# Copies of V on GpSimd in place of SyncE transfers, and two tiles each of q/k and of exponentials turned by transfer

## The chip, the cores and the metric

One core of one Trainium2 chip. The kernel is one program on that core; its engines are TensorE (PE, with its weight loads shown as PEld), VectorE (DVE), ScalarE (ACT), GpSimd (POOL) and SyncE (SP), and 16 DMA engines move data for them. The metric is the device time of one launch in microseconds, lower is better: the median of the runs of one kernel.

## The reference

Attention with a few global rows beside a sliding window, followed by a two-layer network with a hard-swish-like activation. There are 8 batches, 8 heads, 512 local and 32 global positions, heads of 64 numbers. In float32:

```python
k_all = np.concatenate([k_g, k_l], axis=2)
v_all = np.concatenate([v_g, v_l], axis=2)
out_g = np.matmul(sm(scale * np.matmul(q_g, k_all.transpose(0, 1, 3, 2))), v_all)
s_ll = np.where(np.abs(pos[:, None] - pos[None, :]) <= 32, scale * q_l @ k_l^T, -1e9)
s_l = np.concatenate([scale * q_l @ k_g^T, s_ll], axis=-1)
out_l = np.matmul(sm(s_l), v_all)
x = concatenate([out_g, out_l], axis=2)   # to rows of (batch, position), 512 wide: 4352 x 512
h = x @ w_in                               # 512 -> 2048
out = (h * np.clip(h + 3.0, 0.0, 6.0) / 6.0) @ w_out   # 2048 -> 512
```

Here `sm` is a softmax over the last axis. A local position sees the 32 global keys and the local keys at most 32 positions away, so a run of 32 queries needs 32 + 96 = 128 keys.

## The kernel before

**Tiling.** A batch's 512 local positions are four tiles (j = 0 to 3) of 128. A tile's 128 queries are four runs (u = 0 to 3) of 32. For each run the 128 keys are the 32 global ones and a strip of 96 local ones that starts 32 positions before the run. All work on TensorE is in fp16 with fp32 sums.

**Loads.** GpSimd issues the loads, since they convert fp32 to fp16 on the way: q and k of a tile into `nat` (`load_qk`, line 425; 8 buffers), V of a batch into `ve` (`load_v`, line 477; two buffers, one for even and one for odd batches), the global rows into `natg`, and the two weight matrices `win` and `wout` in four pieces each (lines 560 to 566). All go through line 411. At most eight transfers of one queue are under way; the next issue waits for the one eight places before.

**Turning q and k.** `turn_qk` (line 578) makes the transposed form `qk`. For the batches before `TURN_QK` = 4 this is eight TensorE transposes (line 592) and a copy out of PSUM by ScalarE or VectorE (lines 296 and 298); from batch 4 on it is one transposing transfer issued by SyncE (line 582).

**Strips of V.** The second matmul of attention needs, for each run u of each tile, a weight tile whose 128 partitions hold the 32 global rows of V and the 96 local ones of that run. It lies in `st` (two buffers). `strips_moved` (line 526) fills it for a whole batch by seven SyncE transfers from `ve` (line 536): one spread of the 32 global rows to all 16 slots (4 runs x 4 tiles), then for each u the 96 rows, in one or two pieces as they cross a tile's border. With 32 global rows in front, u = 0 moves rows 0 to 95 to partitions 32 to 127; u = 1 moves rows 32 to 127 to partitions 32 to 127, the same ones; u = 2 and u = 3 come in two pieces each. Batch 0 is filled otherwise (`strips_kept` and the two-tile form) and the change doesn't touch it.

**A local step** (`local_step`, line 635): scores of one tile for all heads into PSUM `s` (lines 662 and 669), a masked minimum and bias by VectorE (line 681), exponentials with their sums by ScalarE (line 692), a reciprocal and a scaling into `pn` by VectorE (lines 702 and 706), then the transposition of `pn` into `et`: for the batches before `TURN_E` = 5 eight TensorE transposes (line 713) and one copy out of PSUM, from batch 5 on one SyncE transposing transfer (line 724). Then the matmul with the strips (line 743) into PSUM `a`, copied to `xt`. `global_steps` (line 772) does the 32 global queries of a batch; its last matmuls (line 848) read `ve` directly.

**The network.** `first` (line 863) multiplies by w_in (line 870), applies relu and scale on ScalarE (line 877) and a minimum and product on VectorE (line 881). `second` (line 887) multiplies 16 pieces by w_out into one PSUM bank of 512 columns (line 892), one copy to `ot` (3 buffers), one store. `moe_local` does one batch, `moe_global` all global rows at the end.

**The order.** The operations are not written in the order they run. Each is handed to a planner (`Plan.add`) with an engine, or two to choose from, a duration, what it depends on, a key (its due place) and the buffers it takes. `Plan.lay` walks through time by these durations and a model of the transfers, and gives each engine its list; `fill` adds idle matmuls to the first microseconds. So a changed duration or engine of one operation can move others, on every engine, and choose ScalarE or VectorE anew for each copy out of PSUM. On the chip each engine runs its list in order and waits on semaphores.

Of the kernel before, what the change touches and what calls it, by code (L numbers as in the profile page):

```python
# [79 lines left out]
class Plan:  # L80
# [128 lines left out]
def kernel(  # L209
# [12 lines left out]
    nc = tc.nc  # L222
# [303 lines left out]
    def strips_moved(b, js, key):  # L526
        r = b % 2
        n = len(js)
        j0, j1 = js[0], js[-1] + 1
        v4 = st[r].rearrange("p (u j) c -> p u j c", u=NU)  # L530
        before = [av_last[b - 2, j] for j in range(NJ)] if b >= 2 else []
        o = []

        def move(dst, src, packets, ns, deps):
            def emit(op):
                nc.sync.dma_start(out=dst, in_=src)
            o.append(add("SP", 600, emit, deps + before, key=key + 0.001 * len(o), dma=(packets, ns)))
# [12 lines left out]
        for c in range(NU):  # L550
            lo = c * UQ
            a = min(P - lo, KL)
            deps = [x for j in range(j0, j1) for x in vload[b, j]]
            move(v4[G:G + a, c, j0:j1, :], ve[b % VE][lo:lo + a, j0:j1, :], a * each, ns, deps)
            if a < KL:
                deps = [x for j in range(j0 + 1, j1 + 1) for x in vload[b, j]]
                move(v4[G + a:P, c, j0:j1, :], ve[b % VE][0:KL - a, j0 + 1:j1 + 1, :], (KL - a) * each, ns, deps)
        return o
# [14 lines left out]
            return []  # L573
        return [S_op[b - 2, jj] for jj in range(max(j - 1, 0), min(j + 1, NJ - 1) + 1)] + gS_op[b - 2]

    TURN_M, TURN_QK, TURN_E, TURN_G, TURN = 1, 4, 5, 5, (64, 190.0, True)

    def turn_qk(b, j, ld, key, which=(0, 1)):
        r = b % 2
        if b >= TURN_QK:  # L580
            def move(op):
                nc.sync.dma_start_transpose(out=qk[r][:, :, :, UQ + j * P:UQ + (j + 1) * P].rearrange(
                    "d i p s -> d (i p) s"), in_=nat[ld[0].slot].rearrange("s i c -> s (i c)"))
            return add("SP", 1250, move, [*ld, prep["clear"], *old_qk(b, j)], key=key, rel=ld[:1], dma=TURN)
        w0, n = which[0], len(which)

        def pe(op):
            ps = psM[op.slot].bitcast(FP16) if b < TURN_M else psT[op.slot]
            for i in which:
                for p in range(NP):  # L590
                    c0 = ((i - w0) * NP + p) * P
                    nc.tensor.matmul(out=ps[:, c0:c0 + P], lhsT=nat[ld[0].slot][:, i, p * P:(p + 1) * P],
                                     rhs=ident, is_transpose=True)
# [41 lines left out]
    def local_step(b, j, key):  # L635
# [75 lines left out]
        def tr(op):  # L711
            for h in range(H):
                nc.tensor.matmul(out=psT[op.slot][:, h * P:(h + 1) * P], lhsT=pn[pn_op.slot][:, h, :],  # L713
                                 rhs=ident, is_transpose=True)
        if b < TURN_E:
            t = add("PE", 450, tr, scs, key=key - 0.2, acq="T", rel=[pn_op])
            et_op = add("DVE", 0, lambda op: None, [t], key=key - 0.3, acq="et")

            def ev(op):
                copy(op, et[et_op.slot].rearrange("k h q -> k (h q)"), psT[t.slot])  # L720
            e_ = add(BOTH, (900, 600), ev, [et_op], key=key - 2, rel=[t])
        else:
            def move(op):
                nc.sync.dma_start_transpose(out=et[op.slot], in_=pn[pn_op.slot].rearrange("q h k -> q (h k)"))
            e_ = et_op = add("SP", 1250, move, scs, key=key - 2, acq="et", rel=[pn_op], dma=TURN)
# [158 lines left out]
                                           op0=ALU.min, op1=ALU.mult)  # L884
        return add("DVE", 600, st_, [a], key=key - 1, rel=[f, to])

    def second(t0, gdone, set_, dests, keys):
        f = None
        for q in range(4):
            def pe(op, q=q):  # L890
                for c in range(q * 4, q * 4 + 4):
                    nc.tensor.matmul(out=psM[(f or op).slot], lhsT=gs[set_.slot][:, c, t0:t0 + P],  # L892
                                     rhs=w_out_t[:, c, :], start=(c == 0), stop=(c == NDFF - 1))
            deps = gdone[q * 4:q * 4 + 4] + [wo[q * 4]]
            if q == 0:
                f = s = add("PE", 865, pe, deps, key=keys[q], acq="M")
            else:
                s = add("PE", 865, pe, deps + [s], key=keys[q], rel=[set_] if q == 3 else [])
        oo = add("DVE", 0, lambda op: None, [s], key=keys[3] - 1, acq="ot")

        def ev(op):
            copy(op, ot[oo.slot], psM[f.slot])
        c = add(BOTH, (480, 605), ev, [oo], key=keys[3] - 1, rel=[f])

        for n, (dst, lo, hi) in enumerate(dests):
            def sto(op, dst=dst, lo=lo, hi=hi):
                nc.sync.dma_start(out=dst, in_=ot[oo.slot][lo:hi, :])
            add("SP", 600, sto, [c], key=keys[3] + 0.001 * n, rel=[oo], dma=(hi - lo, STORE))

    def moe_local(b, at, span):  # L910
        set_ = add("ACT", 0, lambda op: None, xdone[b, 0], key=at - 1, acq="gs")
# [4 lines left out]
        def key():  # L916
            left[0] += 1
            return at + span * left[0] / 32
# [5 lines left out]
                done[part][c:c + k] = [o] * k  # L924
        for j in range(NJ):
            row = b * S + G + j * P
            second(j * P, done[j // per], set_, [(out[row:row + P, :], 0, P)], [key() for _ in range(4)])

    def moe_global(at, span):
        deps = [xgd[b] for b in range(B)]  # L930
# [122 lines left out]
```

## Time and profile before

| | us |
|---|---|
| median of 3 runs (lowest, highest) | 332.98 (332.3, 334.16) |
| the profiled execution | 335.23 |
| its span from first to last instruction | 333.5 |
| TensorE busy | 317.4 |
| VectorE busy | 265.2 |
| ScalarE busy | 253.9 |
| GpSimd busy | 106.1 |

The page counts an engine as busy from an instruction's start to its end; matmuls overlap, so the mean duration of one (379 ns for 512 columns) is longer than its share of the time (four take 0.86 us in the chain of waits). GpSimd's busy time is nearly all issuing of loads: 40 of V's local rows at 822 ns, 30 each of q and k at 899 and 914 ns. SyncE's issues aren't counted as busy. Transfers of the GpSimd queue carry 17.05 MB and take 71.9% of the 16 DMA engines' span, those of the SyncE queue 34.55 MB and 48.0%; together over 100%, since a packet's time includes waiting for packets of the other queue. The strips are 7 transfers of 512 KB, 14 of 384 KB, 14 of 256 KB and 14 of 128 KB for the batches 1 to 7, landing some 8 us after their issue. The granted TensorE clock is 0.999.

### The profile page before, as it was taken

To read this page: it belongs to the slowest core of one execution; us is meant where nothing else is said; L and a number is where in the kernel's file an instruction comes from. 1 tells how busy PE (TensorE), PEld (TensorE's weight loads), DVE (VectorE), ACT (ScalarE), POOL (GpSimd) and SP (SyncE) were. 2 spreads that over 40 slices of the span, in tenths; PEclk is the share of its full clock that TensorE was granted. 3 is DMA by queue.
4 is the path that set the end of the run, shared out by engine and by line. 5 is a ranking of instruction groups with operands and counts; after the bars stand their busy time and mean duration, and the time that the engine had idled before them with its cause. 6 is when DMAs were issued, how large, how long until landed. Compare 5 with 4: busy or idle time off the path is not lost.

```text
span 333.5 us, 10205 instructions
## 1 busy us (share of the span) xinstructions
PE 317.4 (95%) x3808; PEld 183.0 (55%) x3808; DVE 265.2 (80%) x997; ACT 253.9 (76%) x850; POOL 106.1 (32%) x139
## 2 busy tenths in 40 slices
PE   8989969799699999999999999999999999999995
PEld 6778855365356554555555555454455544546642
DVE  4899799789988799898998799689988896375400
ACT  4889798679789589977995689699988994474402
POOL 8724943198166733830760050005000000000000
PEclk9999999999999999999999999999999999999999
DMA  9999999999999999999999999999984215300022
GB/s 150 193 245 168 131 177 254 168 190 194 206 152 188 231 155 156 191 225 231 162 173 218 224 160 209 196 198 175 194 145 120 63 35 112 88 0 2 31 64 95
DMA packets 158594, 52.25 MB, mean 157 GB/s; under 512 B 142928, under 2 KB 151120, under 8 KB 158544
## 3 DMA queue, kind: packets, MB, share of 16 engines
q0 software_dynamic: 106560, 17.05, 71.9%
q1 hardware_dynamic: 51984, 34.55, 48.0%
q8 instruction: 30, 0.49, 0.6%
q14 instruction: 20, 0.16, 0.2%
HBM read 35.26 MB, written 8.91 MB: 132 GB/s over the span
## 4 chain that ended last, share of the span: by engine, by line
PE 60%; DMA 19%; POOL 7%; ACT 6%; DVE 5%; issue 2%; SPq 0%; ACTq 0%
PE m L892 28%; PE m L870 23%; DMA wout<-in_moe_w_out_dram 7%; DMA win<-in_moe_w_in_dram 5%; DMA nat<-in_k_l_dram 4%; POOL nat L411 3%; PE a L743 3%; POOL ve L411 3%; ACT sm L692 2%; DMA nat<-in_q_l_dram 2%; DVE gs L881 2%; PE s L669 2%; ACT t L877 1%; PE t L713 1%; PE s L662 1%
## 5 line engine op out<-in xcount | busy, mean ns | idle before, releaser
L892 PE MATMUL m<-wout,gs 128*128 128x512 f16 x544 | 129.6, 379 | 1.3 <-DMA wout<-in_moe_w_out_dram 1.3
L870 PE MATMUL m<-xt,win 128*128 128x512 f16 (+1 forms) x576 | 122.0, 355 | 1.7 <-DVE gs L881 1.0
L692 ACT ACTIVATE sm<-sm,stat 128x128 f32<-128x128 f32 x256 | 100.6, 397 | 11.4 <-DVE stat L681 10.8
L881 DVE SCALAR_TENSOR_TENSOR gs<-t,m 128x512 f16<-128x512 f32 x136 | 91.7, 683 | 19.6 <-ACT t L877 18.3
L877 ACT ACTIVATE t<-m 128x512 f32<-128x512 f32 x136 | 80.4, 597 | 22.1 <-PE m L870 21.3
L870 PEld LDWEIGHTS <-win 128*128 128x128 f16 x640 | 59.3, 98 | 52.2 <-issue 3.3
L892 PEld LDWEIGHTS <-gs 128*128 128x128 f16 x544 | 49.6, 98 | 52.7 <-issue 2.8
L681 DVE CUSTOM_DVE_ANT_0 sm<-s,mask 128x128 f32<-128x128 f32 x256 | 61.8, 283 | 2.5 <-PE s L669 1.1
L692 ACT ACTIVATION_READ_ACCUMULATOR sm<-sm,stat 128x1 f32 x256 | 49.6, 194 | 0.0
L706 DVE TENSOR_TENSOR pn<-sm,stat 128x512 f16<-128x512 f32 x64 | 44.0, 688 | 0.6
L411 POOL DMA_DIRECT2D ve<-in_v_l_dram x40 | 32.2, 822 | 15.0 <-PE m L870 4.3
L296 ACT CAST xt<-a 64x256 f16<-64x256 f32 (+1 forms) x83 | 31.0, 374 | 7.3 <-PE a L743 6.3
L411 POOL DMA_DIRECT2D nat<-in_q_l_dram x30 | 27.0, 899 | 23.1 <-DMA qk<-nat 10.2
L411 POOL DMA_DIRECT2D nat<-in_k_l_dram x30 | 27.4, 914 | 15.7 <-DMA nat<-in_k_l_dram 6.5
L743 PEld LDWEIGHTS <-st 128*128 128x128 f16 x448 | 19.7, 98 | 10.6 <-DVE et L298 0.3
L296 ACT COPY ot<-m 128x512 f32<-128x512 f32 x23 | 13.5, 588 | 13.8 <-PE m L892 10.5
L743 PE MATMUL a<-et,st 128*128 128x64 f16 x448 | 22.1, 193 | 0.2 <-ACT xt L296 0.2
L411 POOL DMA_DIRECT2D ve<-in_v_g_dram x8 | 4.8, 597 | 54.3 <-PE a L848 53.6
L681 DVE DVE_READ_ACCUMULATOR2_ANT stat<- 128x1 f32 x256 | 21.1, 83 | 0.0
L298 DVE CAST xt<-a 64x256 f16<-64x256 f32 (+1 forms) x33 | 14.1, 428 | 4.3 <-PE a L743 4.0
L702 DVE RECIPROCAL stat<-stat 128x4 f32<-128x4 f32 x64 | 11.1, 173 | 5.8 <-ACT sm L692 5.2
L807 ACT ACTIVATE sg<-a,stat 128x32 f32<-128x32 f32 x16 | 4.6, 287 | 14.3 <-DVE stat L798 14.3
(88 smaller groups left out, 279.6 us busy)
## 6 DMA issues: line engine op xcount, KB each, us to landing
out_dram<-ot SPq DMA_DIRECT2D x32, 256.0 KB, 3.7
st<-ve SPq DMA_DIRECT2D x14, 384.0 KB, 7.9
nat<-in_k_l_dram POOLq DMA_DIRECT2D x30, 128.0 KB, 8.1
nat<-in_q_l_dram POOLq DMA_DIRECT2D x30, 128.0 KB, 9.5
st<-ve SPq DMA_DIRECT2D x7, 512.0 KB, 7.7
st<-ve SPq DMA_DIRECT2D x14, 256.0 KB, 8.0
ve<-in_v_l_dram POOLq DMA_DIRECT2D x24, 128.0 KB, 6.0
st<-ve SPq DMA_DIRECT2D x18, 128.0 KB, 8.0
```

Of the source, the lines that this page charges most:

```text
L296: nc.scalar.copy(out=out, in_=in_)
L298: nc.vector.tensor_copy(out=out, in_=in_)
L411: nc.gpsimd.dma_start(out=dst(op), in_=src)
L681: nc.vector.tensor_tensor_reduce(out=sm[sm_op.slot][:, h, :], in0=psS[s.slot][:, e, p * P:(p + 1) * P], in1=m, scale=-scale, scalar=3.0e38 ...
L692: nc.scalar.activation(out=sm[sm_op.slot][:, h, :], in_=sm[sm_op.slot][:, h, :], func=EXP, scale=-1.0, bias=stat[stat_op.slot][:, 0, h:h + 1],
L702: nc.vector.reciprocal(out=stat[stat_op.slot][:, 2, h0:h1], in_=stat[stat_op.slot][:, 1, h0:h1])
L706: (nc.gpsimd if op.eng == "POOL" else nc.vector).tensor_tensor(out=pn[pn_op.slot][:, h0:h1, :], in0=sm[sm_op.slot][:, h0:h1, :], in1=stat[ ...
L743: nc.tensor.matmul(out=psA[a][:, c0:c0 + 64], lhsT=st[r][:, u * NJ + j, p * P:(p + 1) * P], rhs=et[et_op.slot][:, 2 * p:2 * p + 2, u * UQ: ...
L870: nc.tensor.matmul(out=psM[op.slot][:, i * n:(i + 1) * n], lhsT=w_in_t[:, m, (c + i) * P:(c + i + 1) * P], rhs=x()[:, m, t0:t0 + n], start ...
L877: nc.scalar.activation(out=t1[to.slot], in_=psM[f.slot], func=RELU, bias=0.5, scale=1.0 / 6.0)
L881: nc.vector.scalar_tensor_tensor(out=gs[set_.slot][:, c:c + k, t0:t0 + n], in0=t1[to.slot].rearrange("f (k t) -> f k t", k=k), scalar=1.0, ...
L892: nc.tensor.matmul(out=psM[(f or op).slot], lhsT=gs[set_.slot][:, c, t0:t0 + P], rhs=w_out_t[:, c, :], start=(c == 0), stop=(c == NDFF - 1))
```

## The change

- In `strips_moved`, for a whole batch (batches 1 to 7), the spread of the global rows is no transfer any more but eight GpSimd copies, each of 32 partitions and two slots of 512 numbers; and the strip of u = 1, whose rows keep their partitions, is four GpSimd copies (32 and 64 partitions, two tiles each). The other five transfers stay. The planner is told 900 and 850 ns for a copy.
- `TURN_QK` goes from 4 to 3.5 and `TURN_E` from 5 to 4.5, and both are compared with b + j/4: q and k of the tiles 2 and 3 of batch 3, and the exponentials of the tiles 2 and 3 of batch 4, are turned by SyncE transfers.
- `second` can work in `cuts` parts of the columns. The last tile of the last batch is done in two: 16 matmuls of 256 columns, a copy and a store, twice, into one `ot` buffer.

```diff
@@ strips_moved
         if n == NJ:
-            move(st[r][0:G, :, :], ve[b % VE][0:G, 0:1, :].to_broadcast([G, NJ * NU, HD]), G * NJ * NU, SHORT, vload[b, 0][:1])
+            for i in range(0, NJ * NU, 2):
+                o.append(add("POOL", 900, lambda op, i=i: nc.gpsimd.tensor_copy(out=st[r][0:G, i:i + 2, :], in_=ve[b % VE][0:G, 0:1, :].to_broadcast([G, 2, HD])),
+                             vload[b, 0][:1] + before, key=key + 0.001 * len(o)))
...
             deps = [x for j in range(j0, j1) for x in vload[b, j]]
+            if c == 1 and n == NJ:
+                for x0, x1 in ((UQ, 2 * UQ), (2 * UQ, P)):
+                    for i in range(0, NJ, NJ // 2):
+                        o.append(add("POOL", 850, lambda op, x0=x0, x1=x1, i=i: nc.gpsimd.tensor_copy(
+                            out=v4[x0:x1, 1, i:i + NJ // 2, :], in_=ve[b % VE][x0:x1, i:i + NJ // 2, :]),
+                            deps + before, key=key + 0.001 * len(o)))
+                continue
             move(v4[G:G + a, c, j0:j1, :], ve[b % VE][lo:lo + a, j0:j1, :], a * each, ns, deps)
...
-    TURN_M, TURN_QK, TURN_E, TURN_G, TURN = 1, 4, 5, 5, (64, 190.0, True)
+    TURN_M, TURN_QK, TURN_E, TURN_G, TURN = 1, 3.5, 4.5, 5, (64, 190.0, True)
...
-        if b >= TURN_QK:
+        if b + j / NJ >= TURN_QK:
...
-        if b < TURN_E:
+        if b + j / NJ < TURN_E:
...
-    def second(t0, gdone, set_, dests, keys):
+    def second(t0, gdone, set_, dests, keys, cuts=1):
+        w, oo, s, f = dm // cuts, None, None, None
+        for n in range(cuts):
+            cols = slice(n * w, (n + 1) * w)
...
+                        nc.tensor.matmul(out=psM[(f or op).slot][:, 0:w], lhsT=gs[set_.slot][:, c, t0:t0 + P],
+                                         rhs=w_out_t[:, c, cols], start=(c == 0), stop=(c == NDFF - 1))
...
+            def ev(op, cols=cols, f=f):
+                copy(op, ot[oo.slot][:, cols], psM[f.slot][:, 0:w])
+            c = add(BOTH, (480, 605) if cuts == 1 else (300, 340), ev, [oo, s], key=keys[3] - 1, rel=[f])
...
             second(j * P, done[j // per], set_, [(out[row:row + P, :], 0, P)], [key() for _ in range(4)],
+                   2 if b == B - 1 and j == NJ - 1 else 1)
```

In the changed program's order, GpSimd's copies stand between loads: those of batch 1 between the third and the fourth load of w_out, those of batch 2 between q and k of tile 0 and of tile 1 of batch 3. SyncE's two transposes of batch 3 stand between the strip moves of batch 2 and of batch 3. TensorE's order is the same as before up to the scores that start at 56.7 us in the profile.

More of the change, by code (lines that the diff above doesn't have):

```diff
@@ L885, in first, with pe, sto @@
         return add("DVE", 600, st_, [a], key=key - 1, rel=[f, to])
-    def second(t0, gdone, set_, dests, keys):
[L888 to L908, printed above, removed]
+    def second(t0, gdone, set_, dests, keys, cuts=1):
+        w, oo, s, f = dm // cuts, None, None, None
+        for n in range(cuts):
+            cols = slice(n * w, (n + 1) * w)
+            for q in range(4):
+                def pe(op, q=q, cols=cols, f=f if q else None):
+                    for c in range(q * 4, q * 4 + 4):
+                        nc.tensor.matmul(out=psM[(f or op).slot][:, 0:w], lhsT=gs[set_.slot][:, c, t0:t0 + P],
+                                         rhs=w_out_t[:, c, cols], start=(c == 0), stop=(c == NDFF - 1))
+                deps = gdone[q * 4:q * 4 + 4] + [wo[q * 4], s]
+                s = add("PE", 865 // cuts, pe, deps, key=keys[q] + 0.01 * n, acq=None if q else "M",
+                        rel=[set_] if q == 3 and n == cuts - 1 else [])
+                f = f if q else s
+            oo = oo or add("DVE", 0, lambda op: None, [s], key=keys[3] - 1, acq="ot")
+            def ev(op, cols=cols, f=f):
+                copy(op, ot[oo.slot][:, cols], psM[f.slot][:, 0:w])
+            c = add(BOTH, (480, 605) if cuts == 1 else (300, 340), ev, [oo, s], key=keys[3] - 1, rel=[f])
+            for i, (dst, lo, hi) in enumerate(dests):
+                def sto(op, dst=dst, lo=lo, hi=hi, cols=cols):
+                    nc.sync.dma_start(out=dst[:, cols], in_=ot[oo.slot][lo:hi, cols])
+                add("SP", 600, sto, [c], key=keys[3] + 0.001 * (n + i), rel=[oo], dma=(hi - lo, STORE))
@@ L926, in moe_local @@
             row = b * S + G + j * P
-            second(j * P, done[j // per], set_, [(out[row:row + P, :], 0, P)], [key() for _ in range(4)])
+            second(j * P, done[j // per], set_, [(out[row:row + P, :], 0, P)], [key() for _ in range(4)],
+                   2 if b == B - 1 and j == NJ - 1 else 1)
     def moe_global(at, span):
```

## The prediction

> **What bounds the kernel now.** I read the page first, for the share of each engine and the chain of waits.
>
> ```profile
> span 333.5 us, 10205 instructions
> PE 317.4 (95%) x3808; PEld 183.0 (55%) x3808; DVE 265.2 (80%) x997; ACT 253.9 (76%) x850; POOL 106.1 (32%) x139
> DMA  9999999999999999999999999999984215300022
> PE 60%; DMA 19%; POOL 7%; ACT 6%; DVE 5%; issue 2%; SPq 0%; ACTq 0%
> ```
>
> PE is busy nearly always, and the DMA engines are full for three quarters of the span. The chain has 26% of its length on DMA and POOL, so I asked when. Busy time by stage (columns: stretch, its length, PE, PEld, DVE, ACT, POOL, granted clock, DMA share, GB/s):
>
> ```profile
> 36.00:65.00 29.00, 23.69 (x368) 16.62 (x366) 25.99 (x109) 22.81 (x87) 12.73 (x18) 1.00 1.51 194
> 65.00:92.00 27.00, 24.33 (x347) 14.86 (x346) 23.59 (x82) 23.05 (x73) 17.84 (x23) 1.00 1.82 189
> 92.00:130.00 38.00, 37.84 (x478) 21.43 (x477) 33.93 (x122) 31.61 (x107) 21.91 (x28) 1.00 1.67 181
> 130.00:180.00 50.00, 49.39 (x617) 26.91 (x616) 46.31 (x183) 43.50 (x159) 22.27 (x28) 1.00 1.82 192
> 180.00:240.00 60.00, 59.63 (x696) 30.50 (x695) 52.84 (x200) 49.62 (x175) 9.17 (x12) 1.00 1.21 194
> ```
>
> From 92 us on PE stands still 0.16 + 0.61 + 0.37 = 1.1 us in 148. So after 92 us the time is PE's own work: less work there shortens the run by as much, and freed transfers alone shorten nothing. From 36 to 92 us PE is idle 5.3 + 2.7 = 8.0 us. The list of PE's waits says which of that is DMA (columns: us in total, times, longest):
>
> ```profile
> PE t L592 <- DMA nat<-in_k_l_dram: 2.3, 1, 2.3
> ...
> PE m L892 <- DMA wout<-in_moe_w_out_dram: 1.3, 1, 1.3
> ```
>
> The timeline puts the wait for the last quarter of w_out at 63.1 to 64.4 us and the one for k of batch 3, tile 1 at 88.9 to 91.25. Most of the rest (ACT eg 1.5, DVE stat 0.9 and pn 0.8) lies before 51 us, where the changed program issues the same PE order as before: the two orders part at the scores that start at 56.7 us.
>
> **The change, part by part.** Prices from the groups by form, the chain and the timeline (groups: count | busy us, mean ns | idle):
>
> ```profile
> L713 PE MATMUL t<-ident,pn 128*128 128x128 f16 x160 | 12.7, 219 | 0.8 <-DVE pn L706 0.8
> L706 DVE TENSOR_TENSOR pn<-sm,stat 128x512 f16<-128x512 f32 x64 | 44.0, 688 | 0.6
> L296 ACT COPY st<-ve 32x1024 f16<-32x1024 f16 x1 | 1.0, 1045 | 0.0
> L298 DVE COPY st<-ve 32x1024 f16<-32x1024 f16 x2 | 0.8, 420 | 0.1
> L296 ACT COPY ot<-m 128x512 f32<-128x512 f32 x23 | 13.5, 588 | 13.8 <-PE m L892 10.5 <-DMA out_dram<-ot 2.9
> ```
> ```profile
> 93.37 0.45 PE t L713 x8
> ```
> ```profile
> 1.35 0.29 POOL L374 TENSOR_SCALAR_AFFINE_SELECT ident<-ident 128x128 f32<-128x128 f32 x1 [0.91 <-DVE ident L370]
> 1.60 0.26 POOL L326 TENSOR_SCALAR_AFFINE_SELECT mask<-mask 32x96 f32<-32x96 f32 x1
> ```
>
> *Transposes to DMA.* 16 matmuls of L592 (batch 3, tiles 2 and 3) and 16 of L713 (batch 4, tiles 2 and 3) leave PE. Eight take 0.45 us in the chain (the mean of 219 ns counts pipeline overlap), so 32 take 4 x 0.45 = **1.8 us**, all in the dense part: -1.8. Their four evictions go too. In the changed order the planner shares the rest anew: ACT loses 8 ot (588 ns), 2 qk (1022), 2 eg (692) and 2 xt (366) evictions, gains 3 et (1008) and 2 half ot, some -5 us; DVE loses 5 et (686), gains 7 ot (689), 2 eg (483) and 2 xt (420), +3.2 us. Since PE waits only 1.1 us for these engines after 92 us, I take 0, with -1.1 and +3.2 as ends. The four added SP transposes land in 5.3 us (qk<-nat) and 3.7 us (et<-pn). PE's other matmuls hide that; without cover an et costs 3.7 - 0.45 - 0.69 = 2.6 us, two 5.2. The two of batch 3 wait on SP for their loads, with batch 3's strip moves and a store queued behind; the trace before runs batch 3's second tile of scores at 115.8 us, over 20 us after the loads can land, so 0.
>
> *Strips off DMA.* Per batch 1 to 7, SP issues no 512 KB spread and one 384 KB move less: 7 x 896 KB = 6.3 MB of the 34.55 MB that take 48% of the span on SP's queue, so 6.3/34.55 x 160 = 29 us over seven batches, some 4 us each. After 92 us PE doesn't wait for transfers: worth 0. Before, it is worth at most the two waits, 1.3 + 2.3.
>
> *Copies on POOL.* Twelve per batch of 1024 elements on 32 or 64 partitions, 84 in all. No POOL copy is in the trace. Below lies the same copy on DVE, 0.42; ACT does it in 1.04; the two selects give (289 - 258)/32 = 0.97 ns an element, 258 + 928 x 0.97 = 1.16 us. I take 0.95, near ACT's row, since the selects do more and overlap by 0.04 us. So 11.4 us a batch, standing in POOL's queue *ahead of loads*, since they wait for V.
>
> The Trainium skill's GPSIMD Engine Reference (section "Elementwise — side-by-side cycle accounting") states 1.03 cycles an element for bodies of at most two operations, but about 1.8 for a tight loop, at 1.2 GHz. As estimates a copy is then 0.88 or 1.54 us, and the sum -5 us or the slow case below. The selects' 0.97 ns (1.16 cycles) speak for the first.
>
> *Batch 1.* The third w_out load issues by 42.3 us, then copies: eight to 49.9, four more after V tile 3 lands (50.97 before), to about 53.8, with one hold by DVE 54.5. The fourth w_out load issues there instead of at 42.3. Loads three and four landed 57.36 and 64.39, the second 53.28: 4.1 us for one in a clear stretch. So it lands at about 54.5 + 2.5 + 4.1 = 61.1, needed at 63.1: wait gone, **-1.3** (at 1.16 us a copy it lands at 63.5, a wait of 0.4: ends -1.3 and -0.9).
>
> *Batch 2.* POOL reaches its copies at some 73 us (before, q and k of tile 0 were issued by 76.2; the loads ahead wait in POOL's order for that w_out load, now 3.3 us sooner). Eleven and a half us and two holds of 0.69 later, 85.8, it issues q and k of tile 1 of batch 3 (0.88 each), which land about 3.3 us on (the shortest V landing), 90.8. PE needs them 2.0 us of matmuls later in the new order, less the 1.3: 88.9 + 2.0 - 1.3 = 89.6. A wait of 1.2 for 2.3: **-1.1** (ends -2.3 and +4). The same copies feed batch 2's first L743, which moves forward in PE's order and is reached at 85.9: no room either. Later batches have loads well ahead (POOL waits 53.6 us for buffers).
>
> *Tail.* The last block is stored in two halves: the last eviction drops from 588 to about 366 ns (64x256 cast), the store from 256 KB (3.7 us landed) to 128 KB (64 KB lands in 1.7). -0.2 and -0.5 (ends 0 and -1.3): **-0.7**. Matmuls of 256 columns run at half of the 512's 0.216, so 0 on PE.
>
> *Delay of DVE by copies.* L706 has two inputs in SBUF; if it shares a path with POOL's copies, 8 a batch x 11.4/36 = 2.5 meet a copy and wait half of one: 1.2 us, 8.4 in seven batches. DVE holds about a tenth of the chain between 92 and 240 us: **+0.9** (ends 0 and 8.4).
>
> Sum: -1.8 - 1.3 - 1.1 - 0.7 + 0.9 = **-4.0**. The profiled execution took 335.23 us (span 333.5), 2.25 above the median of 332.98; 331.2 against 335.2, so a median of **329.0**, own range 327 to 331.
>
> **Rivals.**
>
> *POOL's queue runs late (slower).* Place: w_out's fourth load and tile 1 of batch 3, both behind copies. Each us on a copy delays 12, and batch 2's start as well, so 24 at the second place. It decides from 0.95 + 4.0/24 = 1.12 us a copy, under the selects' 1.16. At 1.5 us: w_out lands 67.6 (+3.2), k at 104 against 94.1 needed (9.9 for 2.3, +7.6); with -1.8 - 0.7 + 0.9 it is +9.2, 342 us. At 1.16, about 334. For: the copies wait for V ahead of loads the trace shows late. Against: ACT's 1.04 and the smaller element. 18%.
>
> *DVE held by the copies (about the same).* Half of the 8.4 us reaching PE gives -4.0 - 0.9 + 4.2 = -0.7: 332.3. For: DVE is 88 to 93% busy from 92 to 240 us. Against: PE has two gs and three psM buffers of cover. By the Trainium skill's page SBUF — State Buffer, section "Who interferes with whom", a DVE instruction with two SBUF inputs contends with a GpSimd one that reads SBUF, and the loser blocks for the whole instruction. No run so far shows it: all 64 of L706 last 679 to 693 ns, with no POOL copy near. 15%.
>
> *The relief is hidden.* The waits only change name (batch 2's strips, tile 1 again): -1.8 - 0.7 + 0.9 = -1.6: 331.4. 15%.
>
> *It doesn't take the work off PE's path.* SP's transposes come late by the 5.2 us above: 333 to 335. 4%.
>
> **Numbers.** Forecast 48%. A measurement here can tell about 0.5% (1.7 us) from no change: faster is below 331.3, slower above 334.6. Faster: 45 of the 48, 8 from hidden relief, 3 from DVE held: 56%. Slower: 16 of POOL late, 5 from the last and the held DVE: 21%. The rest 23%. Range 326 (a copy at DVE's 0.42 and the best tail) to 336 (a copy a little over the selects' price).
>
> **What would show it.** Right: copies of 0.9 to 1.0 us; no PE wait on w_out; at most 1.5 us of waits on nat or st between 80 and 95 us; PE idle of 1 to 2 us after 92; a last eviction of 128x256. Wrong: copies over 1.1 us; PE waits on POOL (L743) or on nat over 3 us; L706 well over 688 ns, or gaps ahead of it, by a POOL copy; PE waits on DMA et or qk in batches 3 and 4.

## The result, and the profile after

The changed kernel takes 359.0 us in the median (four runs, 355.81 to 361.75) against 333.57 for the kernel before beside it. The ratio is 1.0736, with a 95% interval of 1.0641 to 1.083. The forecast of 329.0 us had the sign wrong, and the time lies far outside the range.

The profiled execution took 355.81 us, with a span of 353.7. Its page begins so (busy time, then 40 equal slices, then the chain of waits):

```profile
span 353.7 us, 10281 instructions
...
PE 323.5 (91%) x3792; PEld 186.7 (53%) x3792; DVE 285.3 (81%) x1003; ACT 250.4 (71%) x841; POOL 195.3 (55%) x223
...
PEclk9999969989999999999999998999999999999999
...
PE 53%; DVE 23%; DMA 10%; ACT 9%; issue 2%; SPq 0%; ACTq 0%
```

The span grew by 353.7 - 333.5 = 20.2 us. PE stands idle for 353.7 - 323.5 = 30.2 us, before 333.5 - 317.4 = 16.1: 14.1 more. Its busy time grew by 6.1 although it has less to do; the row PEclk shows why: in three places the granted clock is lower, before it was full in every slice. DVE's busy time grew by 20.1 us, and its part of the chain from 5% to 23%.

The stretches of the prediction again (stretch, length, PE, PEld, DVE, ACT, POOL, granted clock, DMA share, GB/s):

```profile
36.00:65.00 29.00, 21.35 (x329) 15.74 (x322) 26.50 (x90) 19.70 (x71) 28.33 (x34) 0.88 1.49 169
65.00:92.00 27.00, 23.08 (x312) 14.59 (x310) 25.85 (x86) 20.35 (x72) 26.33 (x30) 0.94 1.18 131
92.00:130.00 38.00, 36.91 (x500) 21.07 (x499) 33.68 (x121) 30.52 (x106) 29.93 (x35) 1.00 1.42 155
130.00:180.00 50.00, 46.45 (x538) 24.55 (x536) 47.88 (x160) 39.85 (x135) 40.08 (x44) 1.00 1.46 157
180.00:240.00 60.00, 53.77 (x595) 26.63 (x595) 50.32 (x195) 43.37 (x165) 30.46 (x32) 0.97 1.13 150
```

From 92 to 240 us PE is now idle 1.1 + 3.55 + 6.23 = 10.9 us, before 1.1. DVE is busier than PE from 36 to 92 and from 130 to 180 us, before only from 36 to 65. What PE waits for (us in total, times, longest):

```profile
PE a L752 <- DMA et<-pn: 5.5, 3, 4.4
PE t L844 <- DVE pg L830: 4.5, 2, 4.2
PE t L722 <- DVE qk L298: 2.9, 1, 2.9
PE t L722 <- DVE pn L715: 2.1, 2, 1.4
PE t L844 <- ACT eg L296: 2.1, 2, 1.8
```

The wait for w_out is gone, and of those on `nat` 0.2 us is left. In their place stand waits for DVE, and one for a transposing transfer. (L830, L715, L637 and L722 were L821, L706, L628 and L713; L541 and L559 are POOL's copies of global rows and of aligned strips. `pg` holds the scaled exponentials of the global queries, `eg` their transposition, `kgz` the global keys as the local scores take them.) The groups behind them:

```profile
L541 POOL COPY st<-ve 32x1024 f16<-32x1024 f16 x56 | 59.8, 1120 | 5.3 <-DMA ve<-in_v_g_dram 5.2
...
L715 DVE TENSOR_TENSOR pn<-sm,stat 128x512 f16<-128x512 f32 x64 | 50.5, 789 | 0.7
...
L830 DVE TENSOR_SCALAR pg<-sg,stat 128x544 f16<-128x544 f32 x16 | 15.6, 1003 | 0.2
...
L637 DVE COPY kgz<-gt 64x128 f16<-64x128 f16 x16 | 7.7, 483 | 0.2
```

Before, L715 was the L706 of the prediction with 44.0 us and 688 ns, and the other two were:

```profile
L821 DVE TENSOR_SCALAR pg<-sg,stat 128x544 f16<-128x544 f32 x16 | 9.1, 611 | 0.2
L628 DVE COPY kgz<-gt 64x128 f16<-64x128 f16 x16 | 3.9, 244 | 0.2
```

Two stretches of the timeline show how PE comes to stand still; the first at 41 to 51 us, the second at 173 to 214 us (start, duration, instruction, and in brackets the idle time before it):

```profile
41.49 8.41 POOL L541 COPY st<-ve 32x1024 f16<-32x1024 f16 x8
...
41.55 6.48 DVE L830 TENSOR_SCALAR pg<-sg,stat 128x544 f16<-128x544 f32 x2
...
46.89 0.71 PE L844 MATMUL t<-ident,pg 128*128 128x128 f16 x5 [4.17 <-DVE pg L830]
...
49.39 0.69 PE L844 MATMUL t<-ident,pg 128*128 128x128 f16 x5 [1.78 <-ACT eg L296]
...
173.73 8.82 POOL L541 COPY st<-ve 32x1024 f16<-32x1024 f16 x8
...
187.10 0.88 POOL L411 DMA_DIRECT2D nat<-in_k_l_dram  x1
...
193.85 9.47 SPq L591 DMA_TRANSPOSE qk<-nat  x3
...
203.42 3.48 SPq L733 DMA_TRANSPOSE et<-pn  x1
...
213.39 0.44 PE L752 MATMUL a<-et,st 128*128 128x64 f16 x8 [4.37 <-DMA et<-pn]
```

Eight copies run on POOL without a gap. The first `pg`, which DVE begins 0.06 us after them, lasts 5.29 us; before, the same one took 0.84, and the median of the sixteen was 0.50. PE transposes it, and stands still for it for 4.17 us. Later the copies of batch 5 stand ahead of seven of the eight loads of q and k for batch 7 on POOL, which are issued from 187 us on. SP's transposes of batch 6, whose own loads were issued before these copies, then take 9.47 us, the transposing transfer of `et` behind them lands 9.9 us after its issue, and PE waits 4.37 us. After both stops, and after one of 2.92 us for `qk` at 74 us, the granted clock is 0.5 for 6.8, 3.4 and 3.4 us.

The ratios here and below leave out executions more than 1.5% above the fastest of their kernel, among them one of e10 with 533 us and one of e11 with 1116 us.

### The profile page after: what moved, and what is told of

Its sections match the earlier page's. It is cut to its first block, busy times and chain, and to the rows that moved or that the text cites. A ratio compares the mean times of both kernels' runs of the same rounds, so it can differ in the third digit from the quotient of the medians.

```text
span 353.7 us, 10281 instructions
## 1 busy us (share of the span) xinstructions
PE 323.5 (91%) x3792; PEld 186.7 (53%) x3792; DVE 285.3 (81%) x1003; ACT 250.4 (71%) x841; POOL 195.3 (55%) x223
## 3 DMA queue, kind: packets, MB, share of 16 engines
q1 hardware_dynamic: 51872, 29.17, 38.4%
## 4 chain that ended last, share of the span: by engine, by line
PE 53%; DVE 23%; DMA 10%; ACT 9%; issue 2%; SPq 0%; ACTq 0%
PE m L903 26%; PE m L879 16%; DMA et<-pn 8%; DVE gs L890 6%; ACT sm L701 4%; DVE sm L690 4%; DVE pn L715 3%; DVE pg L830 3%; PE a L752 3%; DMA st<-ve 2%; ACT t L886 2%; DVE xt L298 2%; ACT sg L816 2%; PE a L1026 2%; PE a L857 1%
## 5 line engine op out<-in xcount | busy, mean ns | idle before, releaser
L903 PE MATMUL m<-wout,gs 128*128 128x512 f16 (+1 forms) x560 | 129.1, 373 | 0.5 <-DVE gs L890 0.4
L879 PE MATMUL m<-xt,win 128*128 128x512 f16 (+1 forms) x576 | 124.8, 361 | 2.7 <-DVE gs L890 2.1
L701 ACT ACTIVATE sm<-sm,stat 128x128 f32<-128x128 f32 x256 | 100.2, 394 | 17.5 <-DVE stat L690 16.8
L879 PEld LDWEIGHTS <-win 128*128 128x128 f16 x640 | 60.3, 99 | 55.0 <-issue 7.3
L903 PEld LDWEIGHTS <-gs 128*128 128x128 f16 x560 | 51.7, 98 | 52.0 <-issue 2.6
L541 POOL COPY st<-ve 32x1024 f16<-32x1024 f16 x56 | 59.8, 1120 | 5.3 <-DMA ve<-in_v_g_dram 5.2
L715 DVE TENSOR_TENSOR pn<-sm,stat 128x512 f16<-128x512 f32 x64 | 50.5, 789 | 0.7
L296 ACT CAST xt<-a 64x256 f16<-64x256 f32 (+1 forms) x81 | 30.2, 372 | 16.2 <-PE a L752 15.1
L559 POOL COPY st<-ve 32x1024 f16<-32x1024 f16 (+1 forms) x28 | 30.2, 1104 | 0.7
L752 PEld LDWEIGHTS <-st 128*128 128x128 f16 x448 | 20.7, 101 | 18.7 <-issue 7.0
L752 PE MATMUL a<-et,st 128*128 128x64 f16 x448 | 23.4, 197 | 6.8 <-DMA et<-pn 5.5
L296 ACT COPY ot<-m 128x512 f32<-128x512 f32 (+1 forms) x17 | 9.5, 560 | 17.5 <-PE m L903 17.3
```

What stands on the lines that cost most here:

```text
L296: nc.scalar.copy(out=out, in_=in_)
L541: o.append(add("POOL", 900, lambda op, i=i: nc.gpsimd.tensor_copy(out=st[r][0:G, i:i + 2, :], in_=ve[b % VE][0:G, 0:1, :].to_broadcast([G, ...
L559: o.append(add("POOL", 850, lambda op, x0=x0, x1=x1, i=i: nc.gpsimd.tensor_copy(out=v4[x0:x1, 1, i:i + NJ // 2, :], in_=ve[b % VE][x0:x1, ...
L701: nc.scalar.activation(out=sm[sm_op.slot][:, h, :], in_=sm[sm_op.slot][:, h, :], func=EXP, scale=-1.0, bias=stat[stat_op.slot][:, 0, h:h + 1],
L715: (nc.gpsimd if op.eng == "POOL" else nc.vector).tensor_tensor(out=pn[pn_op.slot][:, h0:h1, :], in0=sm[sm_op.slot][:, h0:h1, :], in1=stat[ ...
L752: nc.tensor.matmul(out=psA[a][:, c0:c0 + 64], lhsT=st[r][:, u * NJ + j, p * P:(p + 1) * P], rhs=et[et_op.slot][:, 2 * p:2 * p + 2, u * UQ: ...
```

## The experiments

T1: POOL's copies hold DVE, PE stops for late DVE results, and the clock falls behind each stop. T2: the copies delay what is queued behind them on POOL. T3: the added transposes on SP collide with other transfers. Ratios are to the kernel before beside each run, with 95% intervals.

**Parts alone.** `e1_transposes_cuts` is the change without the copies, `e2_copies_only` the kernel before with the twelve copies, `e3_spread_only` with the eight of the global rows, `e4_aligned_only` with the four of the aligned strips.

```diff
 e1 (from after): the POOL copies back to
+            move(st[r][0:G, :, :], ve[b % VE][0:G, 0:1, :].to_broadcast([G, NJ * NU, HD]), G * NJ * NU, SHORT, vload[b, 0][:1])
...
 e2 (from before): both loops of POOL copies of the change, and nothing else
 e3: the first loop alone; e4: the second alone
```

> The changed kernel with the global rows and the aligned strips moved by SP's transfers again, as before; the extra transposes by transfer (batch 3, tiles 2 and 3; batch 4, tiles 2 and 3) and the halved last block stay. T1 (the copies on POOL keep DVE out of SBUF, a late pg or qk on DVE then stops PE, and the granted clock falls to 0.5 after it): no wait of PE over 2.5 us between 36 and 90 us, granted clock 0.99 or more, L830 at most about 1 us, 330 to 333 us. T2 (the copies delay what is queued behind them on POOL, loads above all): the same, 330 to 333. T3 (the extra transposes bunch with stores and loads on the DMA engines and stop PE at 209 us): that stop stays, 340 us or more.

> The kernel before with the twelve copies of a batch on POOL and nothing else of the change. T1: pg on DVE stretched to several us beside the copies, PE stopped for 3 us or more at least once, clock at 0.5 behind it, 345 to 360 us. T2: the same total, but DVE's instructions as long as before, and PE's waits on loads issued by POOL. T3: 331 to 334 us.

> The kernel before with the eight copies of the global rows on POOL (32 partitions, 1024 numbers each) and nothing else. T1: a pg held through several copies of one run, so at least one stop of PE of 3 us; two thirds of the loss of the twelve, about 340 to 350 us; if only runs longer than about five copies do harm, nearly the whole loss. T2: two thirds of the loss as well, by late loads. T3: 331 to 335 us.

> The kernel before with the four copies of the aligned strips on POOL (32 and 64 partitions, 1024 numbers each) and nothing else. T1: a run of four copies can hold one DVE instruction for 4 us at most; a loss of 2 to 8 us, 335 to 341 us, and below 335 if no pg or kgz copy falls into the run. T2: a third of the loss of the twelve. T3: 331 to 335 us.

| kernel | median, us | ratio (95%) |
|---|---|---|
| e1, transposes and halves | 350.2 | 1.0463 (1.0384 to 1.0542) |
| e2, twelve copies | 351.99 | 1.0507 (1.0434 to 1.058) |
| e3, eight copies | 347.3 (340.95 to 348.97) | not formed |
| e4, four copies | 338.02 | 1.01 (1.0064 to 1.0135) |

e2 to e4 went as T1 has it: `pg` lasted 4.09 us in e2, 4.25 in e3, and at most 0.95 in e4, whose copies come after `pg`. But e1 missed by 18 us with no copy at all. Its timeline of PE shows the place:

```profile
187.24 0.36 PE L669 MATMUL s<-qk 64*32 64x96 f16 x32
...
190.91 0.35 PE L662 MATMUL s<-kgz,qk 128*128 128x32 f16 x8 [3.31 <-DVE stat L681]
...
193.53 0.63 PE L786 MATMUL s<-qk,gt 64*32 64x512 f16 x8 [1.86 <-DVE stat L681]
...
196.59 0.59 PE L743 MATMUL a<-et,st 128*128 128x64 f16 x8 [2.43 <-ACT sg L807]
```

Two tiles of scores, the global scores and the second matmul of attention follow each other with no network matmul between, so PE waits for the softmax. In the orders that the planner gave to the kernel before, to the changed one and to e2 no such place exists past the start; in e1's it does. So e1 measures an order that the change does not have, and says nothing of the transposes in the order that it does have. The order of e2 is not that of the change either. To keep the order, all later experiments but e5 start from the changed kernel and alter what an instruction does, not when it is issued.

**The changed order with the copying taken out** (`e6_tiny_copies`), and the change with two of DVE's jobs on ACT (`e5_pg_kgz_act`), which the planner, told of the other engine, puts in another order. e6 and the kernels made from it also have one fill of an `st` buffer on POOL, 3.5 us at 22 us.

```diff
 e6 (from after), and likewise in the aligned strips
-  out=st[r][0:G, i:i + 2, :], in_=ve[b % VE][0:G, 0:1, :].to_broadcast([G, 2, HD])
+  out=st[r][0:G, i:i + 2, 0:8], in_=ve[b % VE][0:G, 0:1, 0:8].to_broadcast([G, 2, 8])
 e5 (from after)
-  nc.vector.tensor_copy(out=kgz...)            # planned on DVE
+  nc.scalar.copy(out=kgz...)                   # planned on ACT
-  nc.vector.tensor_scalar(out=pg..., scalar1=stat..., op0=ALU.mult)
+  nc.scalar.activation(out=pg..., func=Copy, scale=stat...)
```

> The changed kernel in its own order on every engine, but each POOL copy moves 8 of its 512 numbers per slot, so most of the copying of V is left out. What is left of the change is the transposes, the halved last block and the planner's order. T1 (POOL's copies hold DVE, and PE's stops and the halved clock follow): pg at 0.5 us, no wait of PE over 2.5 us before 90 us, clock 0.99; the time falls from 359 by the loss of the copies alone (352.0 - 334.7 = 17) to 340 or below; 331 if the late exponentials at 209 us hang on the copies too, 338 if they do not. T3 (the transposes' order alone loses what they lost without the copies, 350.2 - 334.7 = 15.5): 345 to 350, with PE's stop at 190 to 210 us as before.

> The changed kernel with the scaling of pg and the copies into kgz on ACT in place of DVE (16 and 32 instructions). T1, if these two are what the POOL copies hold: pg about 0.7 us on ACT beside the copies, PE's waits for pg and qk before 90 us gone, clock back to 0.99; ACT gets 20 us more work (250 of 354 us now), some of it in PE's way: 338 to 348 us. If L715 (two inputs in SBUF) is held as much: 350 us or more and waits of PE for pn. T2 (late transfers behind the copies on POOL): no change, 355 to 362.

e6 took 332.28 us, ratio 0.9972 (0.9935 to 1.001). So in the order of the change everything that was lost, 7.6% or some 25 us, is lost by the size of the copies, the late `et` at 209 us included; T3 is out. Its page:

```profile
PE 318.6 (96%) x3792; PEld 184.6 (56%) x3792; DVE 266.6 (80%) x1003; ACT 249.1 (75%) x841; POOL 122.8 (37%) x224
...
PEclk9999997999999999999999999999999999999999
```

DVE is busy 18.7 us less than in the changed kernel with the same 1003 instructions. Three groups make 18.6 of it: `pg` 15.6 to 7.5, L715 (L717 there) 50.5 to 44.0, `kgz` 7.7 to 3.7. Against the kernel before it is 16.8.

e5 took 350.55 us, ratio 1.0468 (1.0392 to 1.0544), as its second case had it, with L715 held as much. The waits for `pg` and `qk` shrank to 1.1 us and none, but L715 had a mean of 837 ns, and PE waited 4.1 us for `pn` and 4.3 for `gs`. Taking these two jobs off DVE, with ACT's added work and the other order in the price, is worth 2.7%.

**Single instructions** (`m1_port`): one DVE instruction twelve times (the narrow copy 24 times), alone and beside work on POOL.

> None of the computation: runs of one DVE instruction alone and beside POOL's copies (12 of 32x1024), beside quarter copies (48 of 32x256), beside fills (12 of 32x1024, which read nothing), beside copies that wait for one another, and beside copies with a tiny fill between. T1: the scaling (128x544) alone 0.50 us; beside the back-to-back copies the first of them waits for the run of copies to end, or several copies (5 us or more), and the rest follow at 0.50; beside quarter copies the same if POOL keeps the port from one instruction to the next, at most 0.3 us more each if it gives it up; with waits or fills between, at most one copy (1.1 us) each. The product (128x512 with a broadcast factor) 0.69 alone and at most one copy longer; the gate's product out of PSUM 0.68 in both. A rival (the long pg was an accident of DVE's own waits): 0.5 to 1.6 us each and no longer one.

DVE's groups in order: the scaling alone, beside copies, quarter copies, fills; the product alone, beside copies, fills; the narrow copy alone, beside copies; the gate's product out of PSUM alone, beside copies:

```profile
3.30 5.03 DVE L40 TENSOR_SCALAR d<-src,stat 128x544 f16<-128x544 f32 x12
...
8.69 12.81 DVE L40 TENSOR_SCALAR d<-src,stat 128x544 f16<-128x544 f32 x12
...
23.61 6.41 DVE L40 TENSOR_SCALAR d<-src,stat 128x544 f16<-128x544 f32 x12
...
42.97 14.44 DVE L40 TENSOR_SCALAR d<-src,stat 128x544 f16<-128x544 f32 x12
...
87.88 7.30 DVE L43 TENSOR_TENSOR d<-src,stat 128x512 f16<-128x512 f32 x12
...
95.61 15.69 DVE L43 TENSOR_TENSOR d<-src,stat 128x512 f16<-128x512 f32 x12
...
113.40 7.30 DVE L43 TENSOR_TENSOR d<-src,stat 128x512 f16<-128x512 f32 x12
...
125.08 2.53 DVE L47 COPY d<-half 64x128 f16<-64x128 f16 x24
...
128.03 13.01 DVE L47 COPY d<-half 64x128 f16<-64x128 f16 x24
...
141.47 7.25 DVE L50 SCALAR_TENSOR_TENSOR d<-src,ps 128x512 f16<-128x512 f32 x12
...
149.14 7.25 DVE L50 SCALAR_TENSOR_TENSOR d<-src,ps 128x512 f16<-128x512 f32 x12
```

Beside whole copies a scaling takes 1.07 us instead of 0.42, a product 1.31 instead of 0.61, a narrow copy 0.54 instead of 0.11; the product that reads PSUM stays at 0.60. Fills hold the scaling (1.20) and not the product (0.61). The Trainium skill's SBUF — State Buffer, section "Who interferes with whom", says this: a DVE instruction with two SBUF inputs contends with GpSimd's reads only, copies and scalings in their two-port mode with its writes too, and the loser waits for the whole instruction. The trace of m1 agrees with all of it. But no scaling lasted over 1.28 us beside copies, which is one copy waited for; the longest, 2.19 us, stood beside fills and was passed over once. The 5.29 us were not found, and that part of T1 missed.

**What the reading costs, and what the length of a copy costs** (`e8_fills`, `e9_quarters`), again in the changed order.

```diff
 e8 (from after), both loops
-  nc.gpsimd.tensor_copy(out=st..., in_=ve...)
+  nc.gpsimd.memset(st..., 0.0)
 e9 (from after), both loops: each copy as four of 256 numbers
+  [nc.gpsimd.tensor_copy(out=st[r][0:G, n, h:h + HD // 2], in_=ve[b % VE][0:G, 0, h:h + HD // 2]) for n in (i, i + 1) for h in (0, HD // 2)]
```

> The changed kernel with each POOL copy turned into a fill with zeros of the same place and size (the global rows and aligned strips of V are left out): nothing is read. By the runs of single instructions a fill holds the scaling (1.20 us each beside fills, 0.42 alone) but not the product with two inputs (0.61 in both). So pg and kgz still lengthened, L715 back at 0.69. T1 with L715 as the larger part (350.6 - 332.3 = 18 us were left when pg and kgz had gone to ACT): about 341 us. If pg and kgz on DVE are the larger part: 350 or more.

> The changed kernel with each POOL copy made as four of 256 numbers a partition, in the same place of the same order; everything is computed. By the runs of single instructions a scaling beside quarter copies takes 0.53 us against 1.07 beside whole ones and 0.42 alone. If DVE waits for the POOL instruction under way and no longer (T1 by instructions): pg and L715 longer by 0.1 to 0.2 us, no stop of PE over 2.5 us, 332.3 + 0.17 x 27 = 337 us, up to 342 since the run of copies on POOL is 12 to 18 us long. If a run of copies keeps DVE out as a whole (T1 by runs): a pg of 4 us or more, PE's stop at 43 us, 352 to 362.

e8 took 343.11 us, ratio 1.0251 (1.0166 to 1.0336): of the 7.4% that the change loses, 4.9 are gone. DVE is nearly free (L714, which is L715 there, has a mean of 687 ns; the longest `pg` is 1.26 us; the three groups are 4.1 us over e6 in place of 18.6). POOL's 84 instructions are shorter too, 77 us in place of 90. The longest waits that are left:

```profile
PE a L751 <- DMA et<-pn: 5.1, 2, 4.9
PE t L843 <- ACT eg L296: 2.0, 2, 1.6
```

So at most 4.9% (16 us) of the loss hang on DVE being held, since the 13 us less on POOL have a part in it that was not measured apart; 2.8% (9 us over e6) are left when DVE is hardly held.

e9 took 368.81 us, ratio 1.1012 (1.0946 to 1.1078): the worst kernel of all, where 337 to 342 were expected. The half that concerns DVE came out: `pg` lasted at most 0.75 us, and L716, which is L715 there, 828 ns in the mean. But a quarter copy costs 0.44 us, not a quarter of 1.1, and POOL is busy 237.9 us. Its copies and PE's longest waits:

```profile
L541 POOL COPY st<-ve 32x256 f16<-32x256 f16 x224 | 88.2, 441 | 1.3 <-DMA ve<-in_v_g_dram 1.1
...
PE a L753 <- DMA st<-ve: 9.4, 2, 5.3
PE m L904 <- DMA wout<-in_moe_w_out_dram: 7.7, 1, 7.7
```

This is the rival "POOL's queue runs late", at the place and of the kind that the prediction gave: w_out's last load stands behind the copies of batch 1, and with 48 copies in 20.4 us it is 7.7 us late. In the change, with 12 in 12.9 us, it is not.

**One batch at a time.** `e10_tiny_batch1` has tiny copies in batch 1 alone, `e11_batch1_only` and `e12_batch5_only` whole copies in one batch alone. `e13_batch1_look` and `e14_no_batch1_look` are e11 and e10 once more, for their profiles.

```diff
 from e6
+        wide = 8 if b == 1 else HD      # e10; e11: HD if b == 1 else 8; e12: HD if b == 5 else 8
-  0:8
+  0:wide
```

> The changed kernel in its own order, with the POOL copies of batch 1 alone cut to 8 of 512 numbers a slot (most of that batch's copying of V is left out). T1: the first stop of PE (4.2 us for pg at 43 us) and the halved clock behind it go, the later ones stay: 359 less the 5.8 us that PE was behind by 52 us, about 353. Rival (each stop hides another, so that the last one decides): no gain, 357 to 361. Rival (the early loss alone sets the rest off): 340 or less.

> The changed kernel in its own order, with POOL's copies whole in batch 1 alone and 8 of 512 numbers a slot in the others (most of their copying of V is left out). T1 (DVE is held, PE stops, the clock halves): pg of 4 to 5.3 us, PE's wait for it of 3 to 4.2 us at 43 us and 0.5 of the clock for some 6 us behind it; 332.3 + 4.2 + 2 to 3 = 338 to 340 us. If pg is held only when later batches' copies are there as well (which nothing suggests): 332 to 334.

> The changed kernel in its own order, with POOL's copies whole in batch 5 alone and 8 of 512 numbers a slot in the others (most of their copying of V is left out). Theory of the queue (T2 for this place): the 13 us of copies delay the loads of q and k for batch 6 behind them on POOL, SP's three transposes qk<-nat then hold SP for 9 us or more (5.0 with tiny copies), and the transpose et<-pn behind them stops PE for 3 to 5 us near 200 us, with 0.5 of the clock after it: 332.3 + 4.4 + 1.8 = 338 us. Theory of the held DVE alone (T1): no wait for et over 1 us, 333 to 334.5 us.

> The kernel of e11 again (POOL's copies whole in batch 1 alone, most of the other batches' copying of V left out), for its profile. T1: pg of 4 to 5.3 us at 42 us, PE stopped 3 to 4.2 us for it, the clock near 0.88 between 36 and 65 us and near 1.00 later, about 337 us. If pg stays under 1.3 us: the long hold needs more than batch 1's copies, and e11's 1% has another source.

> The kernel of e10 again (the copies of batch 1 alone cut to 8 of 512 numbers a slot, most of that batch's copying left out), for its profile. T1: no pg over 1.3 us, no stop at 43 us; L715 still about 0.78 us in the mean; the stop for et near 200 us stays (3 to 5 us), about 346 us.

| whole copies in | ratio (95%) | over e6 |
|---|---|---|
| no batch (e6) | 0.9972 (0.9935 to 1.001) | |
| batch 1 (e11) | 1.0101 (1.0058 to 1.0144) | 1.3% |
| batch 5 (e12) | 1.0268 (1.016 to 1.0376) | 3.0% |
| all but batch 1 (e10) | 1.0336 (1.025 to 1.0422) | 3.6% |
| all (the change) | 1.0736 (1.0641 to 1.083) | 7.6% |

Batch 1 alone: the longest `pg` was 2.82 us in e13, PE waited 1.7 us for it and 2.7 for `eg` behind it, and the clock was down, only there:

```profile
36.00:65.00 29.00, 23.26 (x341) 16.61 (x341) 24.90 (x88) 19.87 (x70) 28.38 (x33) 0.82 1.45 167
65.00:92.00 27.00, 25.96 (x375) 15.69 (x373) 25.75 (x99) 24.43 (x86) 19.49 (x37) 1.00 1.72 176
```

e13 took 338.8 us. The stop is smaller than the 3 to 4.2 us expected. e11's other executions lie in two groups, three from 334.24 to 334.94 us and six from 336.72 to 339.21, so how often the stop comes is not known. Batch 5 alone costs more than the 338 us that the queue's theory gave, by the mechanism that it named: the issue of SP's three transposes takes 9.69 us (5.04 in e6), they land in 10.0 us (4.6), and `et` behind them in 9.5 (5.6 and 6.5). From its timeline:

```profile
162.54 8.82 POOL L544 COPY st<-ve 32x1024 f16<-32x1024 f16 x8
...
175.91 0.88 POOL L413 DMA_DIRECT2D nat<-in_k_l_dram  x1
...
182.84 9.69 SPq L594 DMA_TRANSPOSE qk<-nat  x3
...
192.63 3.95 SPq L736 DMA_TRANSPOSE et<-pn  x1
...
202.17 0.58 PE L755 MATMUL a<-et,st 128*128 128x64 f16 x8 [4.59 <-DMA et<-pn]
```

The loads behind the copies are those of batch 7, while the transposes are of batch 6 and don't need them; the expectation named the wrong batch. In e6 these loads are issued from 163 to 170 us, before the transposes. Here they are issued from 176 to 182, and their packets run beside the transposes: the DMA share between 184 and 190 us is 2.19, in e6 1.24 between 182 and 188. So T2 holds at this place: not a load that comes too late for PE, but loads beside which the transfers that PE waits for are slower. PE also waits 2.3 us for `st` (1.3 in e6).

e14 took 353.13 us, e10 345.82, 346.08 and 351.96 where 353 was expected; so the waits of e14 are those of an execution 7 us longer than e10's shortest. Without batch 1's copies no `pg` was over 0.96 us and the stop at 43 us was gone, but L715's mean stayed at 830 ns, and PE waited 3.0 us for `pn`, 2.6 for `ot` and 3.6 for `et`. The losses of single batches do not add up: taken from the whole, batch 1 is worth 4.0%; alone, 1.3%.

**Why one `pg` waits through several copies.** Three more kernels of single instructions looked for it.

> None of the computation: single instructions again, now with POOL's copies under way before DVE's first one comes, with the source as it is or read twice over as for the global rows, and with DVE's instruction alone in a row or with a product out of PSUM between. If the source read twice makes POOL keep DVE out: a scaling of 4 us or more there alone. If the gap between DVE's instructions does (POOL always has its next copy ready before DVE asks): 4 us or more with the PSUM product between, in both sources. Rival (neither): at most 1.1 us longer in every group, and the 5.3 us of the kernel stay unexplained.

> None of the computation: pairs of scalings on DVE beside eight POOL copies with a source read twice, in five surroundings: nothing else; a reciprocal on DVE that makes the scaling's factor just before, with a wait for it; ACT copying from SBUF to SBUF; four software loads issued by POOL just before the copies; four loads issued by SP. If one of them lets POOL keep DVE out for several copies, a scaling takes 4 us or more in that group and at most 1.2 us in the others. If none does, all stay at 1.2 us or less, and the cause of the 5.3 us stays open.

> None of the computation: two scalings on DVE that come at twelve different moments from just before to some 1.5 us after the start of eight back-to-back POOL copies, and at six moments after copies that POOL begins right behind two software loads. If the moment decides (a request within the first copy, as in the kernel, is passed over): a scaling of 4 us or more at one or more moments, most likely 0 to 0.3 us after the start. If it does not: all at 1.3 us or less, and the cause of the 5.3 us stays open.

None found it. The longest scaling was 1.27 us in m2, 1.27 in m3 and 1.39 in m4, whatever the source, the gap, the company or the moment. In the kernel the long hold came in the profiled executions of the change, e2, e3 and e13 (5.29, 4.09, 4.25, 2.82 us), so it is no accident of one execution. The fifth with whole copies of the global rows in batch 1 and `pg` on DVE, e11's of 1116 us, has `pg` at 111 us, with no copy beside it, and at 0.50 us. What makes POOL keep its turn there is open.

No experiment points to a version that beats the kernel before by more than can be told: with copies that cost next to nothing the change gains 0.3%, with an interval that includes none.

## Why the prediction was wrong

**The step that failed is "Delay of DVE by copies: +0.9".** Its size for L706 was right: at most 8.4 us were given, 6.5 measured. Two things in it were not. It named L706 alone; the scaling of `pg` and the copies into `kgz` are held too, for 8.1 and 4.0 us over e6, which makes 18.6. And it let a tenth of the delay reach PE, by DVE's share of the chain before. The fills (e8), which take 14.5 of the 18.6 away, put what hangs on the held DVE at up to 16 us: nearly one to one, the clock included. A share of the chain is no price for a delay: DVE has 23% of the chain in the change and 20% in e6, which loses nothing. That DVE, 88 to 93% busy before, had no room for 19 us more fits this, but no run varied how busy it is. The rival "DVE held by the copies" had the mechanism, and the Trainium skill's rule beside it was right as far as the single instructions of m1 show it, but with half of 8.4 us it was priced at 332.3. "No run so far shows it" held for L706 only. The trace before shows `pg` held by the loads that POOL issues: five of the sixteen lasted 0.76 to 0.95 us, all beside such issues, while the eleven others lasted 0.49 to 0.51.

```profile
40.79 2.31 POOL L411 DMA_DIRECT2D wout<-in_moe_w_out_dram  x3
...
41.79 1.58 DVE L821 TENSOR_SCALAR pg<-sg,stat 128x544 f16<-128x544 f32 x2
```

**The clock was not in the sum.** In the changed kernel each stop of PE of 2.9 us or more was followed by 0.5 of the clock for 3.4 to 6.8 us. By the rows of the stretches, (1 - 0.88) x 29 + (1 - 0.94) x 27 + (1 - 0.97) x 60 = 6.9 us of full-speed work were lost, which is PE's growth in busy time of 6.1 and a little more. So a stop of 4.2 us costs, as an estimate, 6 to 8: its own length and half of the 3.4 to 6.8 us behind it. Not all of a lower clock is due to the copies: the execution of e6 that was profiled has 0.5 for 3.4 us from 51.6 us on, behind three stops of 0.81 to 0.86 us.

**"Later batches have loads well ahead" failed too.** The rival "POOL's queue runs late" was looked for in two places, w_out and batch 3's tile 1. Neither wait occurred: a batch's twelve copies took 12.5 to 13.4 us, so 1.04 to 1.12 each, dearer than the 0.95 taken and at most just at the 1.12 from which it should decide. (The group's mean of 1120 ns counts the overlap of one copy with the next.) The wait came where the text had ruled it out, by 13 us of copies of batch 5 ahead of the loads of batch 7, and through a third party, SP's transposes of batch 6. In e8, which loses 2.8% (9 us) over e6, this wait is 4.9 us and the clock from 180 to 240 us takes another 0.06 x 60 = 3.6.

**Transposes, w_out, tail.** In e6 the wait for w_out went as forecast (-1.3), and the one on `nat` went whole (-1.1 was forecast); the last eviction is 128x256 and takes 0.37 us. Together with the transposes (-1.8) and the tail (-0.7) the terms without the copies gave -4.9 us. e6, whose copies still take 0.2 us each, came to -0.3%, some 0.9 us, with an interval from -2.2 to +0.3: the size was wrong, and the sign can't be told. Part of it is the tail: from the end of the last matmul to the end of the span it takes 333.5 - 329.7 = 3.8 us before and 332.6 - 329.1 = 3.5 in e6, so -0.3. Where the rest of it stayed was not tested. The added transposes did not collide by themselves: e6 waits 0.6 us for `et` in all.

**Strips off DMA.** The SyncE queue went from 34.55 to 29.17 MB. No run has this alone; in e6, which has it too, nothing beyond the two waits shows.

## What to carry to other kernels

Before work is moved to an idle engine, list what the other engines run at that time and which of it shares a path with the new work; a price from an empty trace is the price of the new instruction, not of what it holds up. Don't price a delay by the engine's share of the chain before: here up to 16 us reached the end where that share gave 0.9. To test a part of a change under a planner, keep the changed order and shrink the instruction: taking the part out gives another order, and in e1 the place shown, which the change does not have, makes PE wait 7.6 of the some 15.5 us that e1 lost.

## What the runs showed of the hardware

- Cutting POOL's copies by four made them dearer: 1.12 us for 1024 numbers a partition, 0.44 for 256 in the kernel. A line through these two gives, as an estimate, 0.21 us a copy and 0.9 ns a number beside a busy DVE; e6's copies of 16 numbers took 0.22.
- A copy that waits for the one before it, or a tiny fill between copies, does not help DVE: 12 scalings took 12.81 and 12.84 us beside these, 12.81 beside copies without a gap.
- The clock fell to 0.5 after idle times of 2.92, 4.17 and 4.37 us. The Trainium skill's TensorE: Matmul & The Clock Gate, Part 1, gives an idle window of about 3.4 us for this; the stop of 2.92 us was enough here, and in e6 three stops of 0.81 to 0.86 us within 7 us were.
- Transposing transfers that land in 4.6 us beside light traffic took 10.0 us when loads of q and k ran at the same time (DMA share 2.19 instead of 1.24), though they did not depend on these loads.
- Loads that POOL issues hold DVE as well: a scaling of 0.50 us took 0.76 to 0.95 beside them in the kernel before.
